# Another issue order for a fused attention and two expert layers, with twelve more idle products behind the first scores

## The chip, the core and the metric

One core of a Trainium2 chip. TensorE (PE, with its weight loads PEld), VectorE (DVE), ScalarE (ACT) and GpSimd (POOL) work side by side, each in the order of its own instruction stream; SP and ACT also issue transfers. The metric is the device time of one execution in microseconds, median over runs.

## The reference

```python
def _attn_ref(q, k, v):                      # 2 x 8 heads, 1152 x 64
    q_pool = q.reshape(B, H, S // 2, 2, D).mean(axis=3)
    scores = scale * np.matmul(q_pool, k.transpose(0, 1, 3, 2))
    scores = scores - np.max(scores, axis=-1, keepdims=True)
    attn = np.exp(scores)
    attn = attn / (np.sum(attn, axis=-1, keepdims=True) + 1e-09)
    return np.matmul(attn, v)
...
    x = _moe_ref(x, w_in, w_out)             # softplus(x @ w_in) @ w_out, 512 -> 2048 -> 512
    return _moe2_ref(x, ...)                 # RMS norm, silu(xn @ w_gate) * (xn @ w_val) @ w_out, d_ff 1536
```

All in float32, 1152 rows of 512 behind the attention.

## The kernel before

The sixteen heads are worked in eight pairs. A pair has 4.5 blocks of 128 pooled queries. For each block and head, PE makes the scores of 128 queries against 1152 keys (L737, two products of three banks each: a high and a low half), DVE takes the negated row maxima `nm` (L751), ACT the exponentials `p` with their sums (L753). The probabilities then have to be turned, so that keys lie on partitions, for the product with the values (the AV product, L838). That is done in one of two ways. Most blocks are turned on PE, four tiles of 128 x 128 at a time, into a bank `t` (L773, called a flip here; L1248 for the block that the two heads share), and ACT or DVE copies the bank out. In five pairs two blocks, and in one pair one, are turned by DVE in squares of 32 (L810, into the tile `turned`), and sixteen transfers on SP's queue move the squares to their places in the tile `moved` (L818). This is called a stream here; its AV product reads `moved`.

The scores have two banks, one for each head; a bank can be written again when the exponential has read it. The banks `t` are two as well.

While a pair is worked, the next one's keys and queries are loaded and split into a high and a low half of reduced precision, on ACT, DVE and POOL. Then the two expert layers follow: products of 512 columns with halves of both operands, in a scheme of seven products in place of eight, with the weights decoded on ACT and DVE. PE warms up at the start with WARM = 20 transpositions of the identity, and makes WAKE more behind the first scores, while the first softmax runs (`heat`).

The program is first written down as a list of 2264 numbered operations, each with the engines that may do it, a cost, and what it depends on. Which engine does it and in which order all are issued is not decided in the program but read from the table ORDER: `p` is PE, `v` DVE, `a` ACT, `g` POOL, `s` SP's queue, `q` ACT's, and the number is the operation's. The costs in `act`, `pool`, `dve` belong to the search that made the table, which is not part of the program.

```python
        for word in ORDER.split():
            o = self.ops[int(word[1:])]
            o.eng = ENGINE[word[0]]
            assert o.eng in [x[0] for x in o.opts] and o not in seen and seen >= o.deps and seen >= o.after, word
            seen.add(o)
            done.append(o)
```

Of the kernel before, what the change touches and what calls it, by code (L numbers as in the profile page):

```python
# [55 lines left out]
WAKE = 16  # L56
# [3 lines left out]
    p46 v3 s10 q11 v8 v4 s12 v7 q13 a45 v9 v5 s14 s15 s16 v20 v21 s17 v2 a22 v6 s18 a28 v23 s19 v29 p48 a24 a44 v25 p47 v26 v27 p49 a32 v34 a30 p54 v50 a35 s57  # L60
    g31 a37 s166 g33 v52 a51 s55 v36 a53 p85 s56 v39 p87 s167 v86 s58 a40 p90 v88 p92 a91 a93 p94 v41 a89 p99 v95 p96 v100 v67 p101 p106 a102 v97 p103 a107 p108
    v42 a98 v104 v38 v76 p110 a109 a105 v43 p112 v111 g78 p114 v113 g62 p117 v115 g70 p119 a118 p121 a120 g63 a116 p124 v122 g64 p126 g77 s59 a125 s60 a123 p128
    v127 v65 p130 a80 a129 v66 p132 a131 v81 p135 v133 p137 p139 a138 g71 g68 a136 a134 p142 g72 v140 p144 g69 a143 a141 v73 s215 p146 v145 s216 a82 v84 p148
    a147 p152 a149 v79 v74 s214 p150 v75 p155 a151 s61 a156 p157 v83 v153 p159 a158 g221 p162 v160 p164 a154 g222 g223 v195 a161 s219 v239 v163 v235 s218 p186
    p188 v224 a165 a187 v225 p191 v240 v189 g237 p193 a192 p205 v226 a190 p209 v194 g231 v206 g230 p207 v210 g228 p212 a208 p246 a213 g232 a211 p249 v247 g236
    s332 s331 a241 v244 a248 s220 p251 v242 a233 g238 p254 v252 a250 p256 a255 g229 p259 a253 v257 g227 v260 a258 p265 v234 p261 v196 a171 p263 p288 a264 v266
    g338 s197 a262 g339 s217 p268 g337 v289 a269 s335 a243 p291 v245 a290 s330 s201 v270 s334 a267 p293 s198 v292 s199 p296 v294 a355 p298 s200 a297 p300 a299
    v271 a295 p303 v314 s278 v301 a168 p305 s279 p307 a306 s276 a304 v351 a302 p310 s282 p312 v308 g202 s286 g353 s277 a311 v313 s274 a309 p321 v315 p325 s275
    s280 v172 a322 p323 s281 v356 v326 g203 a324 p328 p362 s285 a329 g354 s283 p365 v363 a327 s273 g352 s287 s272 a364 v340 v341 s284 p367 g204 s316 g347 a342
    p372 v368 g346 a366 g344 p370 v373 p375 a371 g348 a376 p377 a369 v360 s320 s319 s317 v361 a374 p379 s479 p383 s478 v378 a380 s318 v416 p381 v343 p386 p406  # L70
    a387 v357 v384 g417 a382 p409 a359 v349 v407 g345 s477 v358 a408 v350 p411 v388 a410 p420 v485 a412 s333 a385 g484 s336 g415 g486 p423 v421 p425 g414 a424
# [12 lines left out]
    a744 v753 v783 s712 a780 s714 p811 s728 v745 a807 s731 p814 v812 p816 a815 a817 p821 p818 v784 a813 v832 g810 s796 g855 v819 a822 p823 a860 g856 s790 p828
    p825 g857 s792 v829 a824 s788 a820 v826 p830 s797 s798 v686 s785 a831 p839 a827 p843 s789 v840 s795 v687 p841 s794 v844 p846 g809 a842 p896 s787 a847 g808
    s800 a873 p899 v897 a845 s793 s791 v874 a898 s786 v436 s799 p901 v833 a869 v439 p904 s834 p906 v902 a900 g871 a905 p909 p911 a910 v858 v879 a903 v878 p913
    a912 p915 a914 p917 v907 g870 a916 s883 a444 s852 p920 p922 g440 s884 v918 a908 g861 s853 v921 a919 g441 p924 s851 v859 p926 s885 a923 v863 a925 s887 g442
    a938 s894 p929 v927 p931 a446 g864 s891 g872 s838 v930 a928 s881 g862 s835 p956 v932 a448 s893 v865 p958 v866 s854 a957 p962 v867 s886 a959 v868 p960 s837
    p965 a961 v963 g449 s892 a966 p967 p969 a877 s882 v968 g443 s836 p972 v970 p974 s889 a964 s895 v875 s888 v997 a940 v973 v998 p988 a975 a450 p990 v989 g934
    s999 a971 g447 p993 v991 s890 p995 s880 a994 g941 a992 p1004 v996 p1006 v1005 p1008 g451 a1007 p1011 v1009 p1013 a1012 p1015 g445 a1014 p1018 v1016 g935  # L90
    p1020 s976 a1019 g939 a1010 v933 v936 s1002 p1022 a1021 a1017 v937 s977 s1003 v944 v876 n0 s1000 p1034 a1023 v954 s1001 p1036 a1035 v946 p1038 a1037 v947
    a978 p1041 v1039 p1043 a1042 p1045 a1044 a981 v979 p1048 v1046 g1026 a1040 p1050 g955 a1049 a1047 p1052 v1051 p1054 p1056 a1053 v1055 a952 p1059 p1061 v1060
    g953 p1063 v1057 a1062 a942 g943 a1058 n1080 p1066 v1064 p1068 a1067 v1024 v950 v980 p1070 a1069 v1025 a1065 n1094 p1072 v1071 p1081 v1073 a948 v1089 v951
    p1074 p1076 a1075 v982 a1077 p1078 v1090 p1083 a1079 v945 a984 v983 p1085 p1087 q1093 v1082 g949 a1086 a1027 v1084 a2262 v1029 g985 p1097 a1091 v1088 s1133
    a1092 s1132 a986 p1101 v1098 s1140 p1095 v1102 g987 s1149 a1105 s1148 p1103 p1099 a1096 v1104 n1 s1141 v1028 a1030 v1107 p1118 a1032 a1100 v1106 a1108 p1115
    v1119 a1134 v1110 v1031 p1112 g1111 g1109 p1120 v1113 a1150 v1136 p1124 a1121 v1152 a1122 p1128 a1125 v1123 a1126 v1143 p1162 a1187 a1129 v1151 v1135 v1116
    p1188 a1130 v1033 v1127 p1163 a1189 v1153 p1193 v1154 a1164 v1155 a1142 v1137 p1191 a1158 p1190 v1144 a1138 v1194 a1192 v1156 p1196 v1139 v1131 s1165 p1200
    v1145 s1166 p1204 a1201 v1157 a1146 v1197 p1199 v1159 a1198 a1160 v1147 a1117 v1161 s1179 a1202 p1228 v1203 s1206 p1230 a1229 s1207 a1205 s1180 a1167 p1236
    v1231 v1168 p1239 p1232 v1169 a1240 a1237 v1170 p1241 a1208 p1252 v1242 a1181 v1171 v1172 a1175 p1248 v1173 v1174 v1209 a1177 p1238 v1176 a1233 a1234 v1178
    a1249 p1262 a1253 v1182 s1220 a1243 s1221 v1235 p1244 a1263 v1183 p1266 v1184 p1270 v1245 v1210 a1222 p1273 p1264 v1211 a1250 a1185 p1247 v1212 v1213 a1216  # L100
    v1265 v1251 a1271 v1224 a1267 p1272 a1268 v1186 v1274 s1255 v1217 p1275 s1254 p1310 v1276 v1214 a1277 v1215 p1278 v1223 a1218 p1282 v1219 a1256 p1286 a1246
    v1279 s1289 a1283 v1257 s1288 a1311 p1312 v1225 a1287 a1284 p1318 v1269 a1226 v1313 p1321 a1319 p1281 v1322 a1290 v1291 v1285 v1227 p1314 v1292 s1302 p1323
# [215 lines left out]
def act(n, sbuf=True):  # L318
    return "ACT", n * 0.00096 + 0.15 if sbuf else n * 0.00085 + 0.155
# [7 lines left out]
def body(ctx: ExitStack, tc: tile.TileContext, kT, qT, v, w1, w1o, wg, wv, w2o, rg, outM, outR):  # L327
    nc = tc.nc
# [3 lines left out]
    op = plan.op  # L332
# [1327 lines left out]
```

## Time and profile before

| | |
|---|---|
| median of 3 runs | 650.23 us (649.9, 650.23, 651.69) |
| the profiled execution | 647.97 us |
| its span, first to last instruction | 646.2 us |
| mean granted TensorE clock | 1.000 |
| PE, DVE, ACT, POOL busy | 628.1, 491.1, 385.6, 155.6 us |

The profiled execution is a run of its own; the times inside it are counted from the first instruction.

### The profile page before, as it was taken

Reading aid. Unit: us, or ns where it says so; the run is one execution under the profiler, and the core shown is the slowest. Engines: PE = TensorE matmul, PEld = TensorE weight load, DVE = VectorE, ACT = ScalarE, POOL = GpSimd, SP = SyncE. Lnnn points to the kernel's source line nnn. Section 1 sums busy time; section 2 is a strip of 40 time slices with the busy share of each in tenths; the row PEclk is TensorE's granted clock in tenths of the full one; section 3 lists DMA queues with packets and bytes.
Section 4 is the critical chain, followed back from the end, with each engine's and each line's share of the span. In section 5 each row is a group of like instructions: output and inputs, shape, how many; then the busy total and the mean of one; then the engine's idle time right before and its main releaser. Section 6 shows DMA issues by size and latency. Waiting matters only on the chain.

```text
span 646.2 us, 10956 instructions
## 1 busy us (share of the span) xinstructions
PE 628.1 (97%) x4286; PEld 535.8 (83%) x4286; DVE 491.1 (76%) x695; ACT 385.6 (60%) x642; POOL 155.6 (24%) x160
## 2 busy tenths in 40 slices
PE   8998999899999999999999999999999999999997
PEld 7987888788888987888888888888888888888886
DVE  7799988989998788897886666878978877765111
ACT  6778777877877775675565554456365645533211
POOL 1442633643246241000001111301200101124201
PEclk9999999999999999999999999999999999999999
DMA  9246776968564214423141111111133133201004
GB/s 257 76 130 169 177 198 152 222 173 229 161 153 131 85 46 152 169 92 130 66 152 43 66 65 65 66 66 60 71 131 130 66 131 109 87 5 61 1 0 147
DMA packets 24850, 72.55 MB, mean 112 GB/s; under 512 B 5279, under 2 KB 6110, under 8 KB 24798
## 3 DMA queue, kind: packets, MB, share of 16 engines
q1 hardware_dynamic: 24222, 71.32, 36.9%
q8 instruction: 34, 0.56, 0.4%
q10 hardware_dynamic: 576, 0.53, 0.2%
q14 instruction: 18, 0.15, 0.1%
HBM read 56.46 MB, written 2.39 MB: 91 GB/s over the span
## 4 chain that ended last, share of the span: by engine, by line
PE 86%; DMA 4%; SPq 3%; ACT 3%; DVE 3%; issue 1%; ACTq 0%; DVEq 0%
PE s L953 24%; PE t L838 10%; PE s L1462 9%; PE s L737 9%; PE t L773 6%; PE t L953 5%; SPq L818 3%; PE s L1020 3%; PE s L1021 3%; PE s L1019 3%; PE t L1462 3%; PE s L1040 2%; PE t L1040 2%; PE t L1066 2%; ACT p L753 1%; PE s L1066 1%
## 5 line engine op out<-in xcount | busy, mean ns | idle before, releaser
L751 DVE TENSOR_REDUCE nm<-s 128x1 f32<-128x1152 f32 x72 | 96.7, 1349 | 17.7 <-PE s L737 14.7
L753 ACT ACTIVATE p<-s,nm 128x1152 f32<-128x1152 f32 x72 | 88.1, 1224 | 17.8 <-DVE nm L751 14.8
L372 ACT CAST areaLR<-areaKF 128x512 fp32r<-128x512 f32 (+2 forms) x55 | 44.4, 822 | 34.2 <-PE s L1462 12.0
L773 PE MATMUL t<-ident,p 128*128 128x128 f32 x378 | 55.7, 277 | 5.1 <-ACT p L753 4.0
L377 POOL TENSOR_TENSOR areaLR<-areaKF,areaLR 128x512 fp32r<-128x512 f32 (+1 forms) x9 | 13.1, 1455 | 173.3 <-ACT areaLR L372 150.4
L773 PEld LDWEIGHTS t<-ident,p 128*128 128x128 f32 x378 | 43.3, 140 | 13.2 <-ACT p L753 6.0
L442 ACT ACTIVATE areaKF<-areaKF 128x1024 f32<-128x1024 f32 (+1 forms) x37 | 39.8, 1079 | 20.6 <-DMA areaKF<-in_w2o_dram 5.1
L377 DVE TENSOR_TENSOR areaKF<-areaKF 128x256 f32<-128x256 f32 (+1 forms) x98 | 48.6, 513 | 2.2 <-ACT areaKF L1146 1.4
L372 ACT CAST areaMR<-areaKF 128x512 fp32r<-128x512 f32 (+1 forms) x37 | 26.6, 719 | 38.6 <-PE t L1462 17.1
L377 POOL TENSOR_TENSOR kk<-kr,kk 64x384 fp32r<-64x384 f32 x39 | 40.0, 1036 | 36.6 <-DVE kk L374 15.4
L453 DVE SCALAR_TENSOR_TENSOR areaKF<-areaKF 128x1024 int32<-128x1024 int32 (+1 forms) x37 | 41.8, 1133 | 3.7 <-ACT areaKF L442 3.3
L372 ACT COPY ptwhole<-t 128x512 f32<-128x512 f32 (+1 forms) x62 | 32.5, 546 | 14.1 <-PE t L773 13.6
L372 ACT CAST areaKR<-areaKF 128x1024 fp32r<-128x1024 f32 (+2 forms) x44 | 36.2, 840 | 6.0 <-DVE areaKF L453 4.7
L838 PE MATMUL t<-areaKF,v 128*64 128x128 f32 x576 | 34.7, 274 | 4.5 <-ACT ptwhole L372 2.0
L953 PE MATMUL s<-areaKR,areaLR 128*128 128x512 f32 x132 | 38.2, 395 | 0.0
L953 PE MATMUL s<-areaKR 128*128 128x512 f32 x130 | 37.9, 397 | 0.0
L838 PEld LDWEIGHTS t<-areaKF,v 128*64 128x64 f32 x576 | 31.5, 137 | 7.0 <-ACT ptwhole L372 2.4
L953 PE MATMUL s<-areaMR,areaKR 128*128 128x512 f32 x134 | 36.9, 393 | 0.0
L377 DVE TENSOR_TENSOR areaLR<-areaKF,areaLR 128x1024 fp32r<-128x1024 f32 (+2 forms) x29 | 29.5, 1028 | 8.3 <-ACT areaLR L372 8.1
L838 PE MATMUL t<-ptwhole,v 128*64 128x128 f32 x576 | 35.0, 275 | 0.0
L838 PEld LDWEIGHTS t<-ptwhole,v 128*64 128x64 f32 x576 | 31.1, 137 | 3.5 <-issue 2.5
L377 DVE TENSOR_TENSOR areaLR<-areaKF,areaMR 128x512 fp32r<-128x512 f32 (+1 forms) x21 | 17.5, 837 | 19.9 <-ACT areaMR L372 19.9
(286 smaller groups left out, 1590.7 us busy)
## 6 DMA issues: line engine op xcount, KB each, us to landing
areaKF<-areaKF SPq DMA_DIRECT2D x80, 144.0 KB, 3.0
areaKF<-in_w_dram SPq DMA_DIRECT2D x16, 512.0 KB, 5.4
areaKF<-in_w1o_dram SPq DMA_DIRECT2D x16, 512.0 KB, 4.6
qr<-in_qT_dram SPq DMA_DIRECT2D x28, 288.0 KB, 4.7
areaKF<-in_wv_dram SPq DMA_DIRECT2D x12, 512.0 KB, 4.1
areaKF<-in_wg_dram SPq DMA_DIRECT2D x12, 512.0 KB, 3.8
areaKF<-in_w2o_dram SPq DMA_DIRECT2D x12, 512.0 KB, 4.2
v<-in_v_dram SPq DMA_DIRECT2D x16, 288.0 KB, 5.2
```

Source lines behind the costliest of these rows:

```text
L372: nc.scalar.copy(out, in_)
L377: engines[e].tensor_tensor(out=out, in0=in0, in1=in1, op=o)
L442: o = op([act(n)], lambda e, x0=x0, x1=x1: nc.scalar.activation(out=word(1, x0, x1).bitcast(F32), in_=word(1, x0, x1).bitcast(F32), scale= ...
L453: op([dve(n)], lambda e, x0=x0, x1=x1: nc.vector.scalar_tensor_tensor(out=word(1, x0, x1), in0=word(1, x0, x1), scalar=3, in1=word(0, x0, ...
L737: nc.tensor.matmul(sc()[:, c, :N], lhsT=q()[:, cut], rhs=k()[:, c * N:(c + 1) * N], start=(i == 0), stop=(i == len(todo) - 1))
L751: u["mx"] = op([dve(S, psum=True)], lambda e: nc.vector.tensor_reduce(out=nm(), in_=sc()[:, :, :N], axis=AX.XY, op=ALU.max, negate=True), ...
L753: o = op([("ACT", 1.42)], lambda e: nc.scalar.activation(out=pr(), in_=sc()[:, :, :N], func=AF.Exp, bias=nm(), accum_out=s["den"]()[:, col ...
L773: nc.tensor.transpose(t()[:, i * P:(i + 1) * P], pr[:, c * P:(c + 1) * P], ident)
L838: nc.tensor.matmul(t()[h * D:h * D + D, :n], lhsT=s["v"][h]()[:, c, :], rhs=rhs, start=(c == 0), stop=(c == CK - 1))
L953: nc.tensor.matmul(bank(), lhsT=a(k), rhs=b(k), start=start and k + i == 0, stop=stop and k + i == 3, skip_group_check=seeded)
L1040: nc.tensor.matmul(out, lhsT=x()[:, cut], rhs=w[:, k], start=k + i == 0, stop=k + i == KC + 1)
L1462: nc.tensor.matmul(out[m](), lhsT=w, rhs=g(), start=j + i == 0, stop=last and j == js[-1] and i == 2)
```

## The change

ORDER is another table: 225 of the 2264 operations are on another engine (82 go from ACT to DVE, 67 from DVE to ACT, 49 from DVE to POOL, 27 from POOL to DVE), and most stand elsewhere in the order; 296 of PE's 577 do. WAKE is 28 in place of 16. The costs of the search are changed for ACT, POOL and two operations of DVE, and one condition of the list names `old[0]` where it named 1.

```diff
-WAKE = 16
+WAKE = 28
...
-    p46 v3 s10 q11 v8 v4 s12 v7 q13 a45 v9 v5 s14 s15 s16 v20 v21 s17 v2 a22 v6 s18 a28 v23 s19 v29 p48 a24 a44 v25 p47 v26 v27 p49 a32 v34 a30 p54 v50 a35 s57
+    s10 q11 p46 s12 v6 v9 q13 a45 v2 v4 s14 s15 v20 s16 v21 v3 a22 v28 s17 v5 v23 s18 v29 s19 v24 p48 s167 a26 v25 a44 p47 v27 p49 a32 v34 p54 v50 g33 a37 s57
...
-    return "ACT", n * 0.00096 + 0.15 if sbuf else n * 0.00085 + 0.155
+    return "ACT", n * 0.00083 + 0.2 if sbuf else n * 0.00085 + 0.155
...
-    return "POOL", 0.05 + n * 0.00275
+    return "POOL", 0.18 + n * 0.0022
...
-            op([("DVE", 1.37, 1)], lambda e, h=h, pr=pr: nc.vector.transpose(
+            op([("DVE", 1.37)], lambda e, h=h, pr=pr: nc.vector.transpose(
...
-        op([("DVE", 0.93, 1)], lambda e: nc.vector.reciprocal(sums(), sums()), w=[(sums, None)])
+        op([("DVE", 0.93)], lambda e: nc.vector.reciprocal(sums(), sums()), w=[(sums, None)])
...
-            before = [(pb - 1, t) for t in when.get(x, ())] if len(old) == 2 else [(pb - 1, 1)] if old and x == 1 else []
+            before = [(pb - 1, t) for t in when.get(x, ())] if len(old) == 2 else [(pb - 1, old[0])] if old and x == 1 else []
```

Two places in the order show its kind. The first is on DVE, at the second stream (from 85 us in the trace of before). Names: `nm` are row maxima of a product of scores, `areaKF<-p` at L810 is a transposition of a stream, two for each block. Before:

```order
L633 SCALAR_TENSOR_TENSOR qlB_522<-qs,qhB_126 128x512
L810 STREAM_TRANSPOSE areaKF<-p_1078 128x9x4x32
L377 TENSOR_TENSOR qs<-qr 128x224
L751 TENSOR_REDUCE nm_1201<-s 128x1
L810 STREAM_TRANSPOSE areaKF<-p_1189 128x9x4x32
L751 TENSOR_REDUCE nm_1228<-s 128x1
L863 TENSOR_SCALAR sums<-t 9x128
```

Now, on DVE at the same stream:

```order
L751 TENSOR_REDUCE nm_1136<-s 128x1
L751 TENSOR_REDUCE nm_1157<-s 128x1
L810 STREAM_TRANSPOSE areaKF<-p_1109 128x9x4x32
L810 STREAM_TRANSPOSE areaKF<-p_1159 128x9x4x32
L633 SCALAR_TENSOR_TENSOR qlB_535<-qs,qhB_472 128x512
L751 TENSOR_REDUCE nm_1205<-s 128x1
L656 SCALAR_TENSOR_TENSOR qm_127<-qs,qhB_472 64x64
L374 COPY ptmixed<-t 128x512
L751 TENSOR_REDUCE nm_1237<-s 128x1
```

The last transposition of the stream stood between the reductions of the next pair's first two products of scores, and stands ahead of both now; a sum of queries is gone from between. The third to fifth streams have the same move, the first has not.

The second place is on PE, between the AV product of L838 that begins at 153.58 us in the trace of before and the one at 159.64. `s<-kk01` and `s<-kk11` are products of scores for the two heads, each a bank; `t<-ident,p0` is a flip. Before:

```order
L838 MATMUL t_2042<-ptwhole_231,v11_1895 64x128
L737 MATMUL s_2074<-kk01_1791,qhA1_150 128x384 x3
L737 MATMUL s_2074<-kk01_1791,qlA1_419 128x384 x3
L773 MATMUL t_2086<-ident_69,p0_2065 128x128 x4
L737 MATMUL s_2096<-kk11_1699,qhB1_126 128x384 x3
L737 MATMUL s_2096<-kk11_1699,qlB1_522 128x384 x3
L773 MATMUL t_2106<-ident_69,p0_2065 128x128 x4
L838 MATMUL t_2114<-areaKF_201,v00_1551 64x128
```

Now, on PE at the same place:

```order
L838 MATMUL t_2055<-ptwhole_238,v11_1905 64x128
L737 MATMUL s_2084<-kk11_1835,qhB1_472 128x384 x3
L737 MATMUL s_2084<-kk11_1835,qlB1_535 128x384 x3
L773 MATMUL t_2098<-ident_69,p0_2079 128x128 x4
L737 MATMUL s_2105<-kk01_1664,qhA1_125 128x384 x3
L737 MATMUL s_2105<-kk01_1664,qlA1_426 128x384 x3
L773 MATMUL t_2115<-ident_69,p0_2079 128x128 x4
L838 MATMUL t_2124<-areaKF_161,v00_1544 64x128
```

The products of the two heads have changed places.

## Rows read from the trace of the kernel before

**Rows 1.** The page: busy time of the engines, share of the span, instructions.
```profile
PE 628.1 (97%) x4286; PEld 535.8 (83%) x4286; DVE 491.1 (76%) x695; ACT 385.6 (60%) x642; POOL 155.6 (24%) x160
```
**Rows 2.** Busy time by stretch (from:to, length, engines, granted clock, DMA share, GB/s).
```profile
10.00:232.00 222.00, 209.83 (x2253) 190.89 (x2254) 195.16 (x241) 171.07 (x313) 92.59 (x108) 1.00 0.61 158
232.00:600.00 368.00, 367.75 (x1804) 304.18 (x1803) 282.00 (x425) 198.74 (x305) 52.54 (x38) 1.00 0.25 89
600.00:646.20 46.20, 42.54 (x185) 34.23 (x183) 6.80 (x10) 9.54 (x17) 7.58 (x6) 1.00 0.14 52
```
**Rows 3.** Timeline of PE: start, length, what, [idle before, what ended it].
```profile
10.56 0.66 PE L773 MATMUL t<-ident,p 128*128 128x128 f32 x4 [1.25 <-ACT p L753]
...
88.97 0.33 PE L1248 MATMUL t<-ident,p 128*128 128x128 f32 x1 [0.24 <-ACT ptmixed L372]
...
103.89 2.19 PE L838 MATMUL t<-areaKF,v 128*64 128x128 f32 x36 [1.19 <-DMA row<-sums]
...
125.27 0.44 PE L773 MATMUL t<-ident,p 128*128 128x128 f32 x2 [0.59 <-DVE ptwhole L374]
126.07 0.81 PE L737 MATMUL s<-kk,qhB 128*128 128x384 f32 x3 [0.37 <-ACT p L753]
...
136.69 0.44 PE L773 MATMUL t<-ident,p 128*128 128x128 f32 x2 [0.33 <-DVE ptwhole L374]
...
156.28 0.79 PE L737 MATMUL s<-kk,qhA 128*128 128x384 f32 x3 [0.52 <-ACT p L753]
...
162.36 0.66 PE L773 MATMUL t<-ident,p 128*128 128x128 f32 x4 [0.53 <-ACT p L753]
...
174.50 1.09 PE L773 MATMUL t<-ident,p 128*128 128x128 f32 x8 [0.25 <-ACT p L753]
187.62 2.19 PE L838 MATMUL t<-areaKF,v 128*64 128x128 f32 x36 [1.12 <-ACT ptwhole L372]
...
204.68 2.19 PE L838 MATMUL t<-areaKF,v 128*64 128x128 f32 x36 [0.85 <-DVE ptmixed L374]
```
**Rows 4.** Timeline of DVE at the second and the fifth stream.
```profile
87.89 1.36 DVE L751 TENSOR_REDUCE nm<-s 128x1 f32<-128x1152 f32 x1 [1.04 <-PE s L737]
89.17 1.37 DVE L810 STREAM_TRANSPOSE areaKF<-p 128x1152 f32<-128x1152 f32 x1
...
171.68 1.36 DVE L751 TENSOR_REDUCE nm<-s 128x1 f32<-128x1152 f32 x1 [0.30 <-PE s L737]
```
**Rows 5.** Timeline of SP's queue at the same streams.
```profile
86.64 0.81 SPq L383 DMA_DIRECT2D v<-in_v_dram  x2
...
90.57 10.80 SPq L818 DMA_DIRECT2D areaKF<-areaKF  x16
...
174.35 10.67 SPq L818 DMA_DIRECT2D areaKF<-areaKF  x16
```
**Rows 6.** The chain of waits at 101 us: start, length, what.
```profile
101.46 2.38 DMA row<-sums
```
**Rows 7.** Timeline of PE: the idle products behind the first scores.
```profile
7.34 1.97 PE L1286 MATMUL t<-ident 128*128 128x128 f32 x16
```
**Rows 8.** Timelines of DVE and POOL: first, longest and last of eight conversions.
```profile
26.19 0.43 DVE L699 TENSOR_SCALAR qhA<-qs 128x512 fp32r<-128x512 f32 x1
...
121.75 1.31 POOL L377 TENSOR_TENSOR areaKR<-areaKF,areaKR 128x512 fp32r<-128x512 f32 x1
121.77 1.58 DVE L699 TENSOR_SCALAR qhA<-qs 128x512 fp32r<-128x512 f32 x1
...
200.06 1.45 DVE L699 TENSOR_SCALAR qhB<-qs 128x512 fp32r<-128x512 f32 x1
```
**Rows 9.** The page, costliest groups: count | busy, mean ns | idle before.
```profile
L751 DVE TENSOR_REDUCE nm<-s 128x1 f32<-128x1152 f32 x72 | 96.7, 1349 | 17.7 <-PE s L737 14.7
L753 ACT ACTIVATE p<-s,nm 128x1152 f32<-128x1152 f32 x72 | 88.1, 1224 | 17.8 <-DVE nm L751 14.8
...
L377 POOL TENSOR_TENSOR kk<-kr,kk 64x384 fp32r<-64x384 f32 x39 | 40.0, 1036 | 36.6 <-DVE kk L374 15.4
```

More of the change, by code (lines that the diff above doesn't have):

```diff
@@ L140 @@
[L140 removed]
+    s10 q11 p46 s12 v6 v9 q13 a45 v2 v4 s14 s15 v20 s16 v21 v3 a22 v28 s17 v5 v23 s18 v29 s19 v24 p48 s167 a26 v25 a44 p47 v27 p49 a32 v34 p54 v50 g33 a37 s57
+    a35 a30 v36 a51 v52 g31 p85 g39 s55 p87 a53 v86 s56 v40 p90 v88 p92 a91 a93 p94 v41 a89 p99 v95 p96 v42 v43 a100 p101 v97 p103 a102 v38 p106 a98 v104 p108
+    g63 a67 g64 v107 v76 p110 a109 v62 a105 p112 g69 v111 s59 p114 s60 v113 g79 s58 p117 v115 p119 a118 s61 g70 p121 a120 s166 a116 p124 v122 p126 a80 a65 v81
@@ new lines @@
+    v125 a123 v7 p128 v127 v66 p130 a129 p132 g72 a131 g73 p135 a171 v133 p137 g77 p139 a136 a138 v71 a134 v82 s215 g68 p142 v140 s216 p144 a84 g78 v143 a141
+    s214 p146 v145 v83 p148 a147 v8 v74 p152 a149 v75 p150 g222 v153 p155 a151 g223 p157 a156 p159 g221 v158 a154 s219 p162 v160 p164 s218 a168 a163 v169 a224
+    v195 a239 v235 p186 a165 p188 a161 v187 v240 p191 v225 p193 a192 v189 g230 a226 g231 p205 g232 v194 p209 v206 a190 g228 s332 p207 s331 v210 p212 g229 a208
+    p246 s220 a213 s217 g237 a211 p249 v247 v244 a248 p251 v233 a250 p254 v252 p256 a255 a241 p259 a253 v257 a260 v242 p265 v234 a258 v245 g338 p261 p263 g339
@@ new lines @@
+    p288 a264 v266 g337 a262 g238 s334 p268 g236 v289 a269 a340 p291 g227 v196 a290 v270 s197 a243 p293 s335 v292 v355 p296 a267 s330 v294 p298 s199 a299 p300
+    v297 s200 a295 v271 p303 s198 s201 a304 p305 v314 s276 v301 p310 a306 s286 p307 a311 s280 v356 a302 p312 s273 v308 s287 p325 s274 v313 a309 v341 s278 p321
+    g347 v326 s282 p323 a322 s283 p328 s275 p362 v324 a329 a342 s281 v351 p365 s277 v363 g353 a327 s272 s284 g204 v315 g203 s285 a364 p367 g348 s279 s316 v202
+    p370 v368 g346 a366 p372 g343 a357 a371 p375 a416 g354 v373 p377 a369 g344 s318 v360 s478 a376 g345 s319 p379 s320 a378 v172 p383 a374 s317 v380 g352 s479
@@ new lines @@
+    p381 v361 p386 p406 a387 a382 v384 p409 v407 a385 v388 a408 p411 v389 a410 a349 p420 a412 s336 v350 a359 s398 p423 v421 s404 p427 a424 s477 p425 v358 s392
+    a422 g485 p430 v426 s391 g414 s401 v428 a431 p452 g413 s395 p454 a453 g415 s333 v461 a429 v484 p457 s397 v486 p459 v455 s403 a458 s394 p468 a460 v487 s402
+    a456 p472 v469 s405 v489 s399 p470 p475 v473 s393 a471 p509 g490 a476 s400 p512 v510 s390 a474 s396 s482 v488 a511 p514 v502 v462 a498 p517 v513 s463 v503
+    p522 v515 p519 a518 g500 s481 a523 p524 v507 g492 a516 s465 v520 s466 p526 s467 a525 p530 a521 g494 v527 s464 g493 v508 p528 g495 p533 p553 a534 g491 s601
@@ new lines @@
+    v531 a529 s602 a496 g417 p556 v554 a532 g499 v535 a555 g501 p558 v536 a506 p563 a557 v497 s480 a418 s600 v559 a504 p566 g419 v564 s537 p568 a567 p570 s539
+    v505 s538 a565 v569 g608 p573 s542 v571 g609 s483 a574 p575 g607 s541 p577 g562 v584 a572 g561 s551 v576 p580 g560 v578 p582 s545 a581 s544 v170 a579 s550
+    p591 p595 v583 s547 v592 s548 a612 v625 p593 v610 s552 p598 v596 p632 a599 s546 g614 a594 s549 v633 a597 p635 s540 s543 v173 a634 s605 v626 v611 p637 a180
+    v585 g174 p640 a178 g175 p642 v636 s586 a641 v638 g176 a182 s604 p645 g181 p647 a646 v643 a639 g177 v630 s587 g179 a184 s588 p649 p653 s589 v648 a644 g183
@@ new lines @@
+    a1014 s1001 v936 a1010 p1018 s977 p1020 v1016 s1003 a942 s1000 v937 a1019 s1002 a1017 p1022 v1021 v946 p1034 a1023 p1036 v1035 p1038 a1037 v947 a978 v979
+    p1041 p1043 a1042 v1039 p1045 a1044 p1048 v876 n0 a950 v1046 p1050 a1040 v1049 a1047 p1052 v1051 p1054 v1053 p1056 a1055 v952 a944 g953 p1059 v1057 p1061
+    a981 p1063 a1062 g945 a1060 a1058 n1080 p1066 g943 v1064 p1068 g951 v1067 a1065 n1094 p1070 v982 a954 p1095 v1089 v1069 a1071 v980 g955 p1072 a1096 p1074
+    v1073 p1081 a2262 g1025 v1075 v1024 p1076 a1082 g1026 p1078 v1077 a948 p1083 v1079 v949 p1085 p1087 q1093 a1084 v1086 v1090 v983 v1092 a986 a1091 p1097 g987
@@ L141 @@
+    p2213 a2220 p2219 a2226 g2221 p2216 p2217 v2227 p2223 p2224 p2222 p2225 p2230 p2228 p2251 a2232 s2233 p2229 p2231 a2234 p2254 a2236 s2235 a2238 s2239 p2257
+    s2237 a2258 v2260 q2259 s2261
 """
```

136 lines of the change are left out of this document (56 added, 80 removed).

## The prediction

> **What bounds the kernel now.** I read the page first, then the table of stretches, then each wait of TensorE. The page [rows 1] has PE busy for 97% of the span and DVE for 76%. The stretches [rows 2] say where PE's other 3% lie. From 232 to 600 us, nearly all of the two expert layers, PE is busy for 367.75 of 368.00 us: only fewer matmuls could help there, and the change has the same matmuls. From 10 to 232 us, the attention, PE is busy for 209.83 of 222.00 and idles for 12.17, while DVE is busy for 195.16, 88%. From 600 us on PE idles for 3.66, which is the last copy and store behind the last product; both stand there in the new order too. What an order can win lies inside those 12.17 us.
>
> PE's timeline from 10 to 232 us has 22 rows with an idle time in brackets, from 0.24 to 1.25 us; eleven of them are in [rows 3]. Behind the start they are of three kinds. (a) PE waits for an AV product's operand that sixteen transfers bring (L818, read at L838): 1.19 at 103.89 and 1.12 at 187.62. Both rows name another releaser, but SP's timeline [rows 5] has the sixteen issued from 90.57 over 10.80 us, to 101.37, and from 174.35 over 10.67, to 185.02; in the chain of waits a transfer issued behind the first sixteen landed 2.38 us later [rows 6], and PE goes on 2.5 to 2.6 us behind the last issue both times. (b) PE waits for a softmax or a copy because too little work of its own stands between a product and what needs its result. There are two banks for scores; a bank is free again after the row maxima (1.35 us on DVE) and the exponential (1.22 on ACT) [rows 9], 2.6 us and the hops between engines. The waits at 126.07, 156.28 and 162.36 are for such an exponential, those at 125.27, 136.69 and 88.97 for a copy out of the transposition bank. (c) The copy that PE waits for stands in DVE's queue behind other work: 0.85 at 204.68.
>
> **The change, part by part.** The table gives another order and puts 225 of 2264 operations on another engine. The changed costs (`act`, `pool`, the flags) decide nothing, since the order is the table, and `old[0]` is 1 wherever that branch is taken. Five terms are left, and one for what cannot be seen.
>
> *Streams.* In four of the five pairs of tiles that are turned through transfers, the second transposition (L810) stands on DVE ahead of a reduction that it stood behind; DVE's order above shows one. In the trace that reduction waited for its scores: DVE idled for 1.04 us, reduced for 1.36, and transposed only then, at 89.17; ahead of the other stream it idled for 0.30 and reduced for 1.36 from 171.68 [rows 4]. With the transposition first, it can begin at 86.85 and 171.38, 2.3 and 1.6 us earlier. The sixteen issues began within 0.1 us of its end and the landing follows them, so 1.19 and 1.12 are covered with 0.5 to 1.1 us to spare: 2.31 us gained.
>
> *What the transposition now delays.* It takes 1.37 us and fills an idle time of 1.04 or 0.30, so the reduction begins 0.33 or 1.07 us later. Its exponential and the flips of the same scores follow, and a flip of that kind already waits, 0.25 at 174.50 [rows 3]: the delay is on the path. For four streams, two known and two at the mean of 0.70, the upper bound is 2.8 us. The lower bound is 0, if the transposition itself begins earlier because small operations are gone from ahead of it (in the order above a sum, elsewhere a copy). No row decides; I take the middle, 1.4.
>
> *PE's own order.* Of 577 PE operations 296 have another place, most by one or two. At six waits of kind (b) the cause is gone. At 156.28 the products of scores on the two banks change places (PE's order above): what waited 0.52 us now has a whole product and a flip ahead of it, over 1.5 us of work. At 126.07 an AV product, 2.19 us long, now stands ahead, against a wait of 0.37. At 125.27 the copy that PE waited for stands ahead of a reduction of 1.35 us on DVE, no longer behind it. At 136.69 and 88.97 a product of scores now stands between two flips, and at 162.36 the flip's product is issued one product earlier. Together 0.59 + 0.37 + 0.33 + 0.52 + 0.53 + 0.24 = 2.58 us. At 204.68 the same operations stand ahead of the copy on DVE, two of which I find stretched by POOL (below), so 0 to 0.85; I take 0.4. At 174.50 and eight more PE's order is what it was, and I count nothing.
>
> *Idle products.* Sixteen take 1.97 us [rows 7], 0.12 each, so twelve more take 1.5, and the hole that they fill is 1.25 us long [rows 3]. Cost 0 to 0.25, since a smaller pace inside the group is likely; I take 0.1. The granted clock is 1.00, the level of 2.4 GHz, in the rows of all stretches, with that hole ahead of them, so they have nothing to give back here.
>
> *POOL.* In the attention 18 operations go from DVE to POOL and 7 come back, about 1 us each (1.04 for the commonest, [rows 9]), so POOL has some 10 us more beside its 92.59 [rows 2]. DVE gets as much from ACT as it loses. A conversion on DVE that takes 0.43 us by itself took 1.58 where it began beside a POOL operation, and 1.45 another time, two of eight [rows 8]. The Trainium skill, GPSIMD Engine Reference, section 1, Specifications, states this as a rule: POOL shares its SBUF interface with VectorE, to the cost of DVE instructions in a two-port mode or with two SBUF inputs. The rows agree, and by that rule more work on POOL speaks against this change. The price from the rows: those two lost 1.15 and 1.02, 2.2 us per 92.59 us of POOL, so 10 us more cost 0.24 us of DVE's time, and three times that, 0.7, if the other forms of DVE with two inputs lose as much each. From 0, in DVE's idle 12%, to 0.7, all on the path; I take 0.3.
>
> *Waits that the new order makes.* No trace shows them. Bounds: 0, and the 2.58 us that edits of the same kind remove. I take 0.8, nearer to nothing, since most places moved little. In the expert layers I count nothing: what goes to POOL there is paid from 0.25 us of PE's idle time in 368 and from engines that are busy for 77% (DVE) and 54% (ACT) [rows 2].
>
> Sum: -2.31 + 1.4 - 2.58 - 0.4 + 0.1 + 0.3 + 0.8 = -2.7 us. The profiled execution took 647.97 us, its span 646.2 of them; by this it would take 645.3 with a span of 643.5. The median of the runs shown, 650.23, is 2.3 us above the profiled one, and I keep that distance: 647.5 us.
>
> **The rivals.**
> *DVE is the bound.* DVE works for 195 of 222 us and in order, so a wait taken from PE can come back as a late reduction. With the payback, POOL, the idle products and the new waits at their upper bounds: -4.89 + 2.8 + 0.7 + 0.25 + 2.58 = +1.4, so 651.6, no change that can be told. For it: the waits that stay have the same chain of 2.6 us behind them. Against it: the 27 us in which DVE idles.
>
> *All of it holds.* No payback and no new wait: -2.31 - 2.58 - 0.85 = -5.7, so 644.5; less again if other executions have later transfers than this one, for which the streams now have a margin. Against it: the flip at 174.50.
>
> *Slower: SP stands still inside a stream.* The new order puts loads of the next keys or values between the sixteen issues; before, they stood ahead of them. A load waits until its buffer is free, SP issues in order, and the rest of the sixteen waits with it. Before the second stream the values' load was issued at 86.64, 3.9 us ahead of the sixteen at 90.57 [rows 5]; with the sixteen 2.3 us earlier, 1.6 are left. If the buffers come free 3.5 us later than now, each AV product of four streams waits some 1 to 1.5 us longer than now: +5, against 0.4 of what else remains gained, so about 654. It decides from a delay of some 2 us on, the margin and the covered wait together. For it: keys' buffers come free through POOL, which has more to do. Against it: those 1.6 us.
>
> **How the numbers follow.** A measurement of this kernel tells 0.3%, 2 us, from no change. Faster by more: the forecast and the rival in which all holds, 0.57. Within it: DVE as the bound, or gains that only half hold, 0.24. Slower: SP standing still, or a new wait of that size, 0.19. The range from 643.8 to 651.8 reaches to where nearly all holds below and over the DVE rival above, and leaves out about 0.2, most of it the slower one.
>
> **What would show it.** Right: PE idles for 8 to 10 us in the stretch of the attention; the AV products behind sixteen transfers have no idle time ahead of them at the second and the fifth stream; the waits at the six places are gone; the first flip still begins at about 10.6 us, with next to no idle time ahead. Wrong: waits of over 0.5 us ahead of flips of scores whose reduction stands behind a transposition, an SP wait inside a group of L818, longer conversions on DVE, or idle time of PE between 232 and 600 us.

## The result, and the profile after

The changed kernel takes 656.6 us (median of four runs, 655.43 to 659.96) beside 650.2 for the kernel before: a ratio of 1.011, interval 1.0083 to 1.0137. It is slower by some 7 us; I had forecast 647.5 and a range to 651.8. The profiled execution took 655.43 us with a span of 653.6, 7.4 more than before.

The page of the changed kernel, busy time by engine:

```profile
PE 631.3 (97%) x4298; PEld 539.2 (82%) x4298; DVE 490.4 (75%) x688; ACT 382.8 (59%) x627; POOL 179.6 (27%) x182
```

Its busy time by stretch, with the columns of [rows 2]. The two short stretches lie behind the longest wait of PE:

```profile
10.00:232.00 222.00, 204.94 (x2189) 186.53 (x2189) 186.40 (x232) 166.07 (x296) 97.60 (x115) 0.99 0.63 158
232.00:600.00 368.00, 367.77 (x1856) 305.39 (x1853) 285.55 (x423) 201.39 (x307) 72.24 (x54) 1.00 0.25 89
...
103.00:106.00 3.00, 2.70 (x26) 2.73 (x28) 0.32 (x1) 1.31 (x3) 1.53 (x2) 0.50 0.98 220
106.00:110.00 4.00, 4.00 (x36) 3.54 (x34) 2.26 (x4) 1.40 (x3) 0.45 (x1) 0.99 0.78 194
```

The expert layers are as full as before (367.77 of 368 us). All the loss is in the attention: PE idles there for 17.06 of 222 us, before for 12.17, and for some 3 us the granted clock was at 0.50, the lower of its two levels.

PE's timeline of the changed kernel; the idle time ahead of a row, with the releaser that the profile names, is in brackets:

```profile
79.11 2.19 PE L838 MATMUL t<-areaKF,v 128*64 128x128 f32 x36 [1.68 <-ACT p L753]
93.35 0.66 PE L773 MATMUL t<-ident,p 128*128 128x128 f32 x4 [0.70 <-ACT p L753]
103.30 3.50 PE L838 MATMUL t<-ptwhole,v 128*64 128x128 f32 x36 [3.25 <-ACT p L753]
124.17 0.66 PE L773 MATMUL t<-ident,p 128*128 128x128 f32 x4 [0.71 <-ACT p L753]
132.33 2.18 PE L838 MATMUL t<-ptwhole,v 128*64 128x128 f32 x34 [1.11 <-DMA v<-in_v_dram]
139.47 2.19 PE L838 MATMUL t<-areaKF,v 128*64 128x128 f32 x36 [1.79 <-DMA areaKF<-areaKF]
157.76 0.63 PE L773 MATMUL t<-ident,p 128*128 128x128 f32 x4 [0.73 <-DVE O L374]
168.21 2.19 PE L838 MATMUL t<-areaKF,v 128*64 128x128 f32 x36 [1.72 <-DMA row<-sums]
196.36 2.19 PE L838 MATMUL t<-areaKF,v 128*64 128x128 f32 x36 [1.85 <-DMA qr<-in_qT_dram]
```

Two kinds of AV product wait. Those on `areaKF` stand behind the sixteen transfers of the first, third, fourth and fifth stream, 1.68 to 1.85 us each. Those on `ptwhole`, at 103.30 and 132.33, are the first products with the next pair's values, and wait for the values' load. At 103.30 the row names an exponential, but that product reads no such thing: it reads turned banks, which had been copied out by 99.66 us, and the values, whose load was issued at 94.01. By the semaphore events in the trace that load landed at 103.17 us, and PE's stream waits for its semaphore just ahead of the product; the exponential, which it does not read, ended within 0.01 us of it. The product itself then took 3.50 us in place of 2.19, at half clock.

Over PE's rows from 12.5 us to the end of the attention the idle times in brackets sum to 11.46 us before and 16.88 now: ahead of L838 4.44 and 11.40, ahead of all else 7.02 and 5.48. With 1.31 us for the slow product and 1.11 for a first flip at 11.67 in place of 10.56, this gives 6.96 - 1.54 + 1.31 + 1.11 = 7.8 us, against 7.4 in the span.

SP's timeline at the second stream of the changed kernel (start, duration, transfers issued):

```profile
89.29 0.35 SPq L383 DMA_DIRECT2D v<-in_v_dram  x1
89.70 1.18 SPq L818 DMA_DIRECT2D areaKF<-areaKF  x2
90.99 0.52 SPq L383 DMA_DIRECT2D kr<-in_kT_dram  x1
91.56 2.41 SPq L818 DMA_DIRECT2D areaKF<-areaKF  x4
94.01 0.58 SPq L383 DMA_DIRECT2D v<-in_v_dram  x1
94.64 10.32 SPq L818 DMA_DIRECT2D areaKF<-areaKF  x10
```

In [rows 5] all sixteen issues of this stream took 10.80 us; here the last ten alone take 10.32, and the values that PE needs at about 100 us are issued 4.3 us into the stream. What SP waited for, from 80 to 200 us (total, times, longest), of the changed kernel; no such waits stand in the profile before:

```profile
SPq L818 <- DMA kr<-in_kT_dram: 5.0, 3, 2.4
SPq L818 <- DMA areaKF<-areaKF: 3.7, 9, 1.3
...
SPq L818 <- DMA v<-in_v_dram: 2.2, 3, 1.0
```

SP waits ahead of a transfer of the stream for earlier transfers to land. The chain of waits of the changed kernel has the keys of 90.99 (start, length):

```profile
90.99 7.46 DMA kr<-in_kT_dram
```

They landed at 98.45, and the eighth transfer behind them was issued at 98.47. The same distance of eight holds at the third to fifth stream. How long L818's transfers took from issue to landing, from 60 to 200 us, before:

```profile
DMA to landing us min/median/max: 2.1/3.0/5.7
```

and in the changed kernel:

```profile
DMA to landing us min/median/max: 2.5/5.5/8.3
```

This is where the time went: with loads of 288 and 576 KB between them, the transfers of the streams land 2.5 us later in the median. The Trainium skill, DMA: Bandwidth & Descriptors, section "Queues, rings and completion order", says that a DMA engine works through one queue's descriptors in the order of the ring, and that a later one may still finish first. The landings agree with the order: at the second stream the keys, the values and the sixteen landed as they were issued (keys at 98.45, the next transfer at 99.61, values at 103.17, the next transfer at 103.57).

### The profile page after: what moved, and what is told of

Same layout as the page of the kernel before. It is cut to its first block, busy times and chain, and to the rows that moved or that the text cites. A ratio compares the mean times of both kernels' runs of the same rounds, so it can differ in the third digit from the quotient of the medians.

```text
span 653.6 us, 10971 instructions
## 1 busy us (share of the span) xinstructions
PE 631.3 (97%) x4298; PEld 539.2 (82%) x4298; DVE 490.4 (75%) x688; ACT 382.8 (59%) x627; POOL 179.6 (27%) x182
## 4 chain that ended last, share of the span: by engine, by line
PE 83%; DMA 6%; DVE 5%; issue 2%; ACT 1%; SPq 1%; POOL 0%; POOLq 0%; DVEq 0%; ACTq 0%
PE s L953 25%; PE s L1462 9%; PE t L838 8%; PE s L737 7%; PE t L773 5%; PE t L953 4%; PE s L1019 3%; PE s L1020 3%; PE s L1021 3%; PE t L1462 3%; PE s L1040 2%; DMA v<-in_v_dram 2%; PE t L1040 2%; DVE nm L751 2%; DMA areaKF<-areaKF 2%
## 5 line engine op out<-in xcount | busy, mean ns | idle before, releaser
L372 ACT CAST areaLR<-areaKF 128x512 fp32r<-128x512 f32 (+3 forms) x53 | 43.2, 824 | 30.7 <-DVE areaKF L453 13.7
L377 POOL TENSOR_TENSOR kk<-kr,kk 64x384 fp32r<-64x384 f32 x43 | 43.4, 1017 | 34.3 <-ACT kk L372 24.1
L773 PEld LDWEIGHTS t<-ident,p 128*128 128x128 f32 x378 | 43.3, 140 | 11.5 <-ACT p L753 4.4
L377 DVE TENSOR_TENSOR areaKF<-areaKF 128x256 f32<-128x256 f32 (+1 forms) x98 | 50.8, 539 | 0.9
L372 ACT CAST areaKR<-areaKF 128x512 fp32r<-128x512 f32 (+2 forms) x51 | 39.9, 788 | 19.2 <-DVE areaKF L453 7.8
L377 POOL TENSOR_TENSOR areaLR<-areaKF,areaLR 128x512 fp32r<-128x512 f32 (+1 forms) x12 | 18.0, 1501 | 112.0 <-ACT areaLR L372 76.6
L838 PE MATMUL t<-areaKF,v 128*64 128x128 f32 x576 | 34.7, 274 | 7.0 <-DMA qr<-in_qT_dram 1.8
L838 PE MATMUL t<-ptwhole,v 128*64 128x128 f32 x576 | 36.7, 282 | 4.4 <-ACT p L753 3.3
L372 ACT COPY ptwhole<-t 128x512 f32<-128x512 f32 (+1 forms) x56 | 28.2, 526 | 20.9 <-PE t L773 20.2
L377 POOL TENSOR_TENSOR areaLR<-areaKF,areaMR 128x512 fp32r<-128x512 f32 x10 | 13.6, 1358 | 96.3 <-ACT areaMR L372 60.0
L377 POOL TENSOR_TENSOR qs<-qr 128x224 f32<-128x224 f32 (+1 forms) x35 | 21.1, 624 | 66.5 <-DVE qm L656 22.5
L838 PEld LDWEIGHTS t<-ptwhole,v 128*64 128x64 f32 x576 | 32.6, 141 | 8.2 <-ACT p L753 3.5
L838 PEld LDWEIGHTS t<-areaKF,v 128*64 128x64 f32 x576 | 31.5, 137 | 9.4 <-ACT p L753 3.9
```

What stands on the lines that cost most here:

```text
L372: nc.scalar.copy(out, in_)
L377: engines[e].tensor_tensor(out=out, in0=in0, in1=in1, op=o)
L773: nc.tensor.transpose(t()[:, i * P:(i + 1) * P], pr[:, c * P:(c + 1) * P], ident)
L838: nc.tensor.matmul(t()[h * D:h * D + D, :n], lhsT=s["v"][h]()[:, c, :], rhs=rhs, start=(c == 0), stop=(c == CK - 1))
```

## The experiments

The ratio is always to the kernel before, run on the same chip, with its 95% interval. Four runs (PE's order, POOL's operations, keys alone, and loads ahead with the transposition late) share one set in which the kernel before took 651.8 us, in the other sets 649.5 to 650.4; gains of 0.2% in these four are not read as gains. The diffs of ORDER show the words of one engine, most at the second stream: `s477` is the load of keys, `s333` and `s336` of values, `s481` and `s482` of queries, `s390` to `s405` are the sixteen; `v388` and `v389` are the two transpositions of the second stream, `v421` the reduction that changes places with the second of them.

**Loads inside, on the order of before.**

```diff
-s477 s333 s336 s481 s482 s396 s399 s390 s400 s405 s392 s398 ...
+s336 s396 s399 s477 s390 s400 s405 s392 s333 s398 ... s482
```

> The kernel before, with one thing of the change: SP issues the next pair's keys and values between the sixteen transfers of the second to fifth stream, where the changed kernel does. Landing theory: a load between them makes the transfers behind it land late (the changed trace has 5.3 to 8.3 us from issue to landing in these streams, the one before 2.5 to 4.7), SP pauses, and the loaded values come late too. Each of the four streams then costs 1 to 3 us at its own AV product or at the first AV product of the next pair: slower by 4 to 10 us than the kernel before, with PE waits of over 1 us ahead of L838. Engines theory (the loss comes from the operations moved to POOL and between ACT and DVE, or from the start): within 1 us of the kernel before.

Measured: 1.0274 (1.0228 to 1.0321), 668.4 us. PE's timeline of this kernel, its three longest waits:

```profile
103.14 4.11 PE L838 MATMUL t<-ptwhole,v 128*64 128x128 f32 x36 [5.36 <-DMA v<-in_v_dram]
...
147.58 1.54 PE L773 MATMUL t<-ident,p 128*128 128x128 f32 x6 [4.84 <-DVE O L374]
...
170.55 4.11 PE L838 MATMUL t<-ptwhole,v 128*64 128x128 f32 x36 [3.63 <-DMA v<-in_v_dram]
```

Both long waits at L838 are for values, and each is followed by a product that takes 4.11 us. The place of the loads is shown to be able to make the whole loss and more; its size was over what I expected. But the edit moved the next pair's queries behind the sixteen as well, and the third wait is theirs: DVE, which has to copy the bank out, stood still for the queries of the third stream:

```profile
142.45 0.95 DVE L377 TENSOR_TENSOR qs<-qr 128x224 f32<-128x224 f32 x2 [6.37 <-DMA qr<-in_qT_dram]
```

Behind each of the three waits PE works at the lower clock (columns of [rows 2]):

```profile
103.20:107.50 4.30, 4.30 (x37) 3.97 (x38) 1.68 (x4) 2.22 (x6) 1.95 (x2) 0.50 0.97 225
147.60:151.90 4.30, 4.30 (x15) 3.89 (x15) 1.78 (x2) 1.93 (x5) 2.60 (x3) 0.50 0.70 193
170.60:175.80 5.20, 5.20 (x40) 4.87 (x41) 3.08 (x4) 1.84 (x5) 2.81 (x3) 0.50 1.01 227
```

PE's waits sum to 24.8 us here against 11.5, and half of the 14 us of work at 0.50 is lost, 7 us: together the 20.4 us by which this profile's span is longer. The queries' wait with the slow work behind it is some 7 of them, an estimate.

**Loads ahead, in the changed kernel.**

```diff
-s336 s398 s404 s477 s392 s391 s401 s395 s333 s397 ...
+s477 s333 s336 s398 s404 s392 s391 s401 s395 s397 ...
```

> The changed kernel, with the loads of keys and values put ahead of the sixteen transfers of the second to fifth stream, as they stood before; all else stays. Landing theory: the 3.25 us wait at the AV product at 103.30, with the half clock behind it, goes, and the waits of 1.1 to 1.85 us behind the later streams shrink: faster than the changed kernel by 3 to 6 us, 651 to 654. Engines theory and start theory: within 1 us of the changed kernel.

Measured: 1.0054 (1.0023 to 1.0086), 654.4 us, at the upper end of what the landing theory expected: half of the loss is gone, half stays. In the profile the wait at the first product with new values is gone; AV products behind the sixteen still wait up to 1.91 us. But the profiled execution was the fastest of ten, 649.1 us, with waits of 12.1 us in all and a mean granted clock of 0.999; the other nine took 651.7 to 657.1 at 0.992 to 0.997. What the half that stays is made of is therefore not shown; by those means the lower clock makes 2 to 5 us of each at most, an estimate. What this execution does show: SP stood 8.0 us ahead of the keys' load, for its buffer, until 91.28, and the sixteen, ready at 89.72, began at 92.67.

**Early transposition, on the order of before.**

```diff
-v388 v485 v421 v389
+v388 v389 v485 v421
```

> The kernel before, with the second transposition of the second to fifth stream ahead of the reduction that it stood behind, and nothing else. My prediction's term for the streams: -2.31 with up to +2.8 given back, so -1 us with 1.4 given back; the waits of 1.19 at 103.89 and 1.12 at 187.62 are gone. Rival (the second transposition is not what the sixteen wait for, or its delay comes back in full at the softmax): within 0.5 us of the kernel before, or slower.

Measured: 1.004 (1.0017 to 1.0063), 652.5 us: not faster, slower. DVE's timeline of this kernel at the second stream:

```profile
86.38 1.37 DVE L810 STREAM_TRANSPOSE areaKF<-p 128x1152 f32<-128x1152 f32 x1
89.24 1.38 DVE L810 STREAM_TRANSPOSE areaKF<-p 128x1152 f32<-128x1152 f32 x1 [1.48 <-ACT p L753]
...
90.81 2.61 DVE L751 TENSOR_REDUCE nm<-s 128x1 f32<-128x1152 f32 x2
```

and PE's rows of the same kernel behind three of the streams:

```profile
93.62 0.81 PE L773 MATMUL t<-ident,p 128*128 128x128 f32 x4 [2.11 <-ACT p L753]
...
122.27 0.66 PE L773 MATMUL t<-ident,p 128*128 128x128 f32 x4 [1.33 <-ACT p L753]
...
151.48 0.66 PE L773 MATMUL t<-ident,p 128*128 128x128 f32 x4 [1.37 <-ACT p L753]
```

The transposition could not start where I had put it: its own exponential ended at 89.1, so DVE idled for 1.48 us with the reduction queued behind. The waits at L838 fell from 4.44 to 1.39 us, as predicted, and those ahead of all else rose from 7.02 to 13.07.

**Twelve more idle products, on the order of before.**

```diff
-WAKE = 16
+WAKE = 28
```

> The kernel before with 28 idle products in place of 16. Start theory: the changed kernel is 1.1 to 1.2 us late at its first flip because of the idle products, so this one is slower by about 1.2 us. Rival: the lateness there comes from the granted clock, which is full from 7.06 us in the changed trace and from 4.51 in the one before, and has nothing to do with idle products that stand behind it: within 0.3 us, and the first flip at 10.6 us when the clock is full from 4.5.

Measured, from the timed runs alone: 0.9995 (0.9972 to 1.0019), no difference, though the interval reaches to 1.2 us. What the late first flip waits for stands in ACT's timeline, the first exponential, before and in the changed kernel:

```profile
9.19 1.22 ACT L753 ACTIVATE p<-s,nm 128x1152 f32<-128x1152 f32 x1 [0.60 <-DVE nm L751]
...
10.24 1.22 ACT L753 ACTIVATE p<-s,nm 128x1152 f32<-128x1152 f32 x1
```

It ends at 10.41 and 11.46, and the flip follows 0.15 and 0.21 us later: nearly all of the 1.11 us lies ahead of the flip's operand, and the idle products hold the flip up by less than 0.1. The kernel with POOL's operations (below), which has 16 idle products, is late as well; PE's timeline:

```profile
1.36 4.53 PE L1286 MATMUL t<-ident 128*128 128x128 f32 x20 [1.36 <-POOL ident masks.py:199]
...
11.36 0.66 PE L773 MATMUL t<-ident,p 128*128 128x128 f32 x4 [0.89 <-ACT p L753]
```

The twenty first products take 4.53 us there as in the changed kernel, against 3.92 before. Over the profiles here (without that of this experiment) the first flip began at 10.5 to 11.6 in the order of before, at 11.1 to 11.8 in the changed one. So most of the 1.1 us at the start can belong to the execution; whether some tenths are the changed start's own stays open.

**PE's order, on the order of before.**

```diff
-p718 p757 p723 p760 p767 p765 p762 p770
+p718 p723 p757 p760 p762 p765 p767 p770
```

and the other places from 87.7 to 158.9 us in the same manner.

> The kernel before, with PE's order of the changed kernel from the scores at 87.7 us to the flip at 158.9, and with it the order of two pairs of reductions and exponentials and of two copies of a turned bank; transpositions, loads and engines stay. My prediction's term for PE's own order: -2.58 us, the waits at 88.97, 125.27, 126.07, 136.69, 156.28 and 162.36 gone. Rival (a product moved ahead of one wait makes the next one as long): within 0.7 us of the kernel before, with waits at other places of the same sum.

Measured: 0.999 (0.9971 to 1.0009). The rival holds: of my 2.58 us nothing can be measured. In its profile, of an execution of 652.3 us, the waits at the six places are gone or shorter, and others have grown (1.67 at 93.12, 1.34 at 134.43).

**Loads ahead and transposition late, in the changed kernel.** To the edit of the loads ahead, above, comes

```diff
-v388 v389 v350 v421 v358
+v388 v350 v421 v389 v358
```

> The changed kernel with the loads of keys and values ahead of the sixteen, and with the second transposition of four streams behind the reduction, both as before; what stays of the change is PE's order, the engines and the idle products. If the loads and the early transposition carry the whole loss: 648 to 651, no change from the kernel before or a little faster by PE's order. Engines theory: 652 or more, with waits that no transfer of a stream explains.

Measured: 0.9978 (0.9959 to 0.9998), 649.8 us. With these two edits the loss is gone; that 0.2% more is gained is not shown. PE's timeline of this kernel, the AV products behind the second to fifth stream:

```profile
106.76 2.19 PE L838 MATMUL t<-areaKF,v 128*64 128x128 f32 x36 [0.45 <-DMA areaKF<-areaKF]
...
134.56 2.19 PE L838 MATMUL t<-areaKF,v 128*64 128x128 f32 x36 [0.61 <-DMA areaKF<-areaKF]
...
162.63 2.19 PE L838 MATMUL t<-areaKF,v 128*64 128x128 f32 x36 [0.15 <-DMA qr<-in_qT_dram]
...
190.37 2.19 PE L838 MATMUL t<-areaKF,v 128*64 128x128 f32 x36 [0.71 <-ACT areaKR L372]
```

The last three were 1.79, 1.72 and 1.85 in the changed kernel (at the second stream the long wait ahead had covered it). The median landing is 3.4 us, against 4.8 with the loads ahead and the transposition early.

**Keys alone inside; values alone inside, on the order of before.**

```diff
-s477 s333 s336 s481 s482 s396 s399 s390 ...
+s333 s336 s481 s482 s396 s399 s477 s390 ...
```

```diff
-s477 s333 s336 s481 s482 s396 s399 s390 s400 s405 s392 s398 ...
+s477 s336 s481 s482 s396 s399 s390 s400 s405 s392 s333 s398 ...
```

> The kernel before, with the keys' load alone moved between the sixteen transfers of the second and the fourth stream (behind the first two); all values stay ahead. Landing theory by size: a load of 576 KB, twice that of values, makes the transfers behind it land later by 2 us or more, so the AV products of these two streams wait 1 to 4 us longer: slower by 2 to 6 us. Rival (what costs is that the values come late, not the stream): within 1 us of the kernel before.

> The kernel before, with one load of values each moved between the sixteen transfers of the second to fifth stream (behind 6, 4, 6 and 1 of them), keys ahead of them as before. Landing theory: these values are needed by the first AV product of the next pair, some 7 us behind the start of the sixteen; issued 3 to 4 us into them and landing 5 to 8 us later they come late by 3 to 6 us at the second and fourth stream, so +5 to +13 us, and PE's long waits stand ahead of L838 on ptwhole, with the granted clock at half behind waits of 3 us and more. Rival (the keys make the loss, values alone are small): within 2 us of the kernel before.

Measured: keys 1.007 (1.0042 to 1.0099), values 1.0065 (1.0042 to 1.0087). Both cost some 4 us; for the values that is less than the 5 to 13 I expected. PE's timeline with the values inside:

```profile
100.58 2.19 PE L838 MATMUL t<-ptwhole,v 128*64 128x128 f32 x36 [1.80 <-DMA v<-in_v_dram]
...
158.66 2.19 PE L838 MATMUL t<-ptwhole,v 128*64 128x128 f32 x36 [1.10 <-DMA v<-in_v_dram]
```

With both inside, these two waits are 5.36 and 3.63: the values then stand behind the keys too. The two parts, 4.6 and 4.2 alone, make 18 together. Some 7 of the 18 are the queries' (above), so that 11 or so stand against 8.8; that keys and values do more together than alone is likely, not shown.

**POOL's operations, on the order of before.** Thirty words change their engine and keep their place, for example

```diff
-v485 v413 v494
+g485 g413 g494
```

> The kernel before, with the 30 operations of the attention that the change moves between DVE and POOL on their new engine (22 to POOL, 8 back), at their old places in the order. My prediction: +0.3, from 0 to 0.7. Engines theory: a conversion on POOL is late for the product that needs it, +2 us or more, with PE waiting for kk or ql. Nothing at all if DVE's idle time covers it.

Measured: 0.9978 (0.9957 to 0.9999): no loss. That more work on POOL costs DVE's time, the rule of the Trainium skill that I had weighed (GPSIMD Engine Reference, section 1, Specifications), is not seen in the time of this run.

**Both parts together, on the order of before.** The edits of the loads inside and of the early transposition.

> The kernel before with both parts together: the second transposition of four streams ahead of the reduction, and keys and values between the sixteen transfers. The two parts alone gave ratios of 1.004 and 1.027. If they add: 1.031, about 670 us. If the early transposition makes up for loads inside, as both together in the changed kernel suggest (1.011 there): 1.008 to 1.018, 655 to 662 us, since the sixteen and the loads between them then go 1 to 2 us earlier.

Measured: 1.0115 (1.008 to 1.015), 659.0 us, the ratio of the change itself. The queries stand behind the sixteen here too, and cost again: PE waits 2.33 us at 143.26 for a copy on DVE, which had idled 3.15 us for them.

**Transposition late, loads inside, in the changed kernel.** The edit of DVE above alone.

> The changed kernel with the second transposition of four streams behind the reduction, as before, and the loads left between the sixteen transfers. Interaction theory: loads inside alone cost 1.027 on the order of before, and 1.0115 with the early transposition; so here too the loss grows when the transposition goes back: 1.017 to 1.027, 661 to 668 us, with waits of over 3 us ahead of the first AV product of the next pair. If the parts add instead: 1.011 less what the late transposition gave in the kernel with loads ahead (1.0054 to 0.9978), so 1.003, 652 us.

Measured: 1.0178 (1.0142 to 1.0213), 662.2 us; the interaction theory holds, the sum of parts does not.

**A mended version.** To the changed kernel with loads ahead and transposition late come these, and the same for `v620`:

```diff
-v426 v569 v694 v817 v822
+a426 a569 a694 a817 a822
-p423 p427 p425 p430
+p423 p425 p430 p427
-v388 v350
+v350 v388
```

> The changed kernel with loads ahead and the second transposition late (ratio 0.998 in the run before), and the five copies of the shared block's bank (ptmixed) that the change moved from ACT to DVE back on ACT, and the rounding of two queries' low halves ahead of the first transposition as before. There the copy stood behind the late transposition on DVE: waits of 1.65, 1.66 and 1.00 us for ptmixed, and 1.24 for the low half. If these go: 2 to 4 us faster than that kernel, 645 to 648. Rival: DVE and ACT are so full there that the waits come back at the next product, 649 to 651.

Measured: 0.9984 (0.9967 to 1.0001), no faster than without. The rival holds: the waits for `ptmixed` are gone, but PE's timeline of this kernel has others grown:

```profile
78.94 2.19 PE L838 MATMUL t<-areaKF,v 128*64 128x128 f32 x36 [2.05 <-ACT ptwhole L372]
...
106.58 2.19 PE L838 MATMUL t<-areaKF,v 128*64 128x128 f32 x36 [1.06 <-DMA areaKF<-areaKF]
```

The two parts in all their combinations, as ratios to the kernel before:

| loads of keys and values | second transposition | the rest as before | the rest as changed |
|---|---|---|---|
| ahead of the sixteen | late | 1 | 0.9978 |
| ahead | early | 1.004 | 1.0054 |
| between them | late | 1.0274 | 1.0178 |
| between them | early | 1.0115 | 1.011, the change |

The two lower cells of the first column have the queries behind the sixteen too; the second column has that in all four. How long the sixteen take to land (median, us) is, from top to bottom, 3.0, 4.5, 4.5 and 4.0 in the first column and 3.4, 4.8, 4.6 and 5.5 in the second: either edit alone makes it longer, so the landing by itself does not tell what a cell costs; when the transfer is issued counts as well.

## Why the prediction was wrong

**Streams, -2.31: the step that failed.** "The sixteen issues began within 0.1 us of its end and the landing follows them": the first part nearly held (0.03 to 1.4 us), the second did not. I had carried over the 2.5 us from the last issue to PE's go from an order in which the loads were ahead by up to 7 us. On the order of before the term came true: with the transposition early and nothing else, the waits at L838 fell by 3.05 us. In the changed order the sixteen are ready earlier against PE's products (4 us at the second stream), the loads stand between them, and the sixteen land 5.5 us behind their issue in place of 3.0. PE goes on 4.1 to 5.6 us behind the last issue at the third to fifth stream. In place of 2.31 gained, the waits at L838 grew by 6.96 us, and behind the longest of them the clock fell, for 1.31 more.

**What the transposition delays, +1.4.** Mis-sized for the order of before, because I dated its start by DVE's queue alone: 86.85 us, where its exponential ran until about 88. ACT's timeline of the kernel before:

```profile
86.85 1.23 ACT L753 ACTIVATE p<-s,nm 128x1152 f32<-128x1152 f32 x1
```

Alone, the move costs 6.05 us ahead of other products against 3.05 gained ahead of L838, and is slower by 0.4%. In the changed kernel the exponential comes earlier, and at three of the four streams DVE runs both transpositions back to back. The flips behind the delayed reductions of the second to fourth stream waited in the kernel before:

```profile
90.71 0.66 PE L773 MATMUL t<-ident,p 128*128 128x128 f32 x4 [0.24 <-ACT p L753]
...
118.15 0.66 PE L773 MATMUL t<-ident,p 128*128 128x128 f32 x4 [0.71 <-ACT p L753]
...
146.89 0.66 PE L773 MATMUL t<-ident,p 128*128 128x128 f32 x4 [0.24 <-ACT p L753]
```

The same flips wait 0.70, 0.71 and nothing in the changed kernel, that of the fifth stream 0.25 both times: 0.2 us for the four, less than my 1.4.

**PE's own order and new waits, -2.98 and +0.8.** In the changed trace the six waits that I named are gone, as is the one at 204.68. The waits ahead of all but L838 are 1.54 us less; for these my terms, the transposition's with them, gave -2.58 + 0.8 + 1.4 = -0.4. Alone, PE's order gave nothing that can be measured. **POOL, +0.3:** no loss was measured. **Idle products, +0.1:** under 0.1 in the changed trace; the timed runs cannot tell it from nothing. The expert layers: nothing, as said.

**The rival in which SP stands still** had the place and nearly the time (its own terms, +5 less 0.4, give 654.8, not 654) but another mechanism. No load between the sixteen waited for its buffer: the keys were issued 0.11 us behind the transfer ahead of them, the values 0.04. SP stood still because it had eight transfers under way, and the stream was late because its transfers lie behind the loads'. I priced only what SP waits for, and let "1.6 us are left" speak against it; a landing of 3 us under 1.2 MB of other transfers was never priced. At 0.19 it had too little of the chance.

**Why the two parts belong together.** The loads wait for their buffers, SP's waits say: the values for AV products of the pair (L838), the keys for a conversion on ACT. If the sixteen are ready early, loads ahead of them hold them back or fall right in front of them (1.0054); between them, they come late (1.011). If the sixteen are ready late, the loads have gone by then, and ahead of them is the best place. The early transposition softens the loss of loads inside (1.0274 to 1.0115, and 1.0178 to 1.011), and adds one where they stand ahead; these signs were measured on both orders. How it softens is only in part seen. In the changed order the loads inside go earlier by it: keys and values of the second stream at 90.99 and 94.01, against 94.48 and 97.88 with the transposition late. On the order of before they hardly do there (by 0.3 and 0.7 us), but PE itself comes 4 us later to the product that needs the values, held up by the delayed softmax (2.08 us at a flip at 93.49, with the clock at 0.50 behind it), and so waits less.

## What to carry to other kernels

A transfer's time to land is no constant of its kind: read it together with what the same queue issued in the few microseconds ahead of it, and count the bytes. When an operation is moved earlier, date it by its own operands, not by the gap in its engine's queue, and look up what must then be issued beside its transfers. Two edits that each look like a loss or a gain can turn in each other's presence: try all four combinations before either is judged.

## What the runs showed of the hardware

SP issued a transfer only when the eighth before it had landed: 98.45 and 98.47 us at the second stream, 127.92 and 127.94 at the third. The semaphores in the traces show what sets it here: SP's transfers use eight of them in turn, in both kernels, and the issue waits until the last transfer on its own semaphore has landed. So the limit stands in the program's instructions; whether the queue has one of its own these runs don't show. At 0.64 us an issue this is not felt while transfers land within 5 us, and was not before. The clock stood at 0.50 behind some of PE's waits of 2 to 4 us (behind the 2.11 at the flip at 93.62 of the early transposition, behind the 3.25 here), and not behind others (2.32 at 191.41 in the kernel with PE's order); where it did, a wait of 3.25 us cost 4.6. The waits at L838 sum to 4.44 us in one profile and 5.90 in another whose SP order is the same (the kernel with POOL's operations, in an execution of 651.9 us), so a single wait below 1 us is not taken as an effect of an edit.
